# Moving the transposing DMAs of batches 2 and 3 from positions 4 and 5 to positions 8 and 9 of a step, in six steps of eight

## The chip, the cores and the metric

The kernel runs on one core of one Trainium2 chip. The metric is the device time of one execution in microseconds (us), from the inputs in device memory to the output written there. The core has a matrix engine (PE, with a separate path for its weights, PEld), a vector engine (DVE), a scalar engine (ACT), a general engine (POOL), an engine that only issues DMAs (SP), and 16 DMA engines that all queues share. Each engine works through its own instructions in the order of the program; semaphores tie the engines together. SP, POOL and ACT each issue DMAs. In this program all DMAs that transpose are issued by SP.

## The reference, cut to what matters

Two layers follow one another. The first is block-sparse attention on q, k and v of shape (4 batches, 8 heads, 768 rows, 64 columns), float32. Rows form 24 blocks of 32. A block of queries sees its own block and the two beside it, the first and the last block, and three blocks drawn for it; the first and the last block see everything.

```python
scores = scale * q @ k.T                      # scale = 1/sqrt(64)
scores = where(mask, scores, -1e9)            # mask: window, first/last block, 3 sampled blocks
attn = softmax(scores)
x = (attn @ v)                                # -> (4 * 768 tokens, 8 * 64 = 512)
```

The second is a gated feed-forward layer on the 3072 tokens, with 512 columns in and out and 1536 in the middle:

```python
xn = x / sqrt(mean(x * x) + 1e-6) * rms_g
out = (silu(xn @ w_gate) * (xn @ w_val)) @ w_out    # float32
```

## The kernel before, in words

**Batch 0** is computed densely, in three groups of 256 tokens, at the start. It plays no part in the change, except that its feed-forward work of the third group still runs when the next phase begins.

**Batches 1 to 3** are cut into 18 chunks of 128 query rows, six to a batch: chunks 0 to 5 are batch 1, 6 to 11 batch 2, 12 to 17 batch 3. The last chunk of batches 1 and 2 holds the edge blocks. The main loop has 19 steps. Step i has ten positions, 0 to 9. At a position the loop first issues the jobs listed for it (`do(n, f)` puts job f at position n) and then calls `position()`, which issues a share of the feed-forward pieces that wait in a list. So the order of all instructions is written out by hand, and an engine that waits holds up everything that stands behind it in its own order.

In step i stand, among others:

- positions 0 to 2: the product with V and the normalisation of chunk i-1 (`values`, `normalise`, L660 and L690);
- positions 1 onwards: the scores of chunk i (`scores`, L625);
- position 4: `squares` (ACT), 5: `rms_power` (POOL), 7: `x_scaled` (L714) of chunk i-1. `x_scaled` scales the chunk's rows on DVE and then lets SP issue a transposing DMA that puts them into `xg`, the moving operand of the feed-forward products (L726). Four chunks (4, 8, 16 and 17) are transposed by PE instead;
- positions 0 to 9: the gathers for chunk i+1. POOL copies sampled keys at position 0, ACT at positions 1 to 9, both on L497; DVE gathers queries and keys from position 3 on (L512 to L515 and L483 to L488); POOL issues the gathers of V by indirect DMA at position 2 (L524). All of these but the gathers of V read `KT` and `QN`, the transposed keys and queries of a batch.

**The transposed keys and queries.** `KT` and `QN` exist twice, for even and for odd batches. Those of batches 2 and 3 are made by `turn_by_dma` (L466): for a pair of heads, SP issues one transposing DMA that reads a tile of 128 partitions by 768 bf16 (192 KB) and writes a tile of the same size.

```python
def turn_by_dma(b, pr, which):
    src = (qbf if which else kbf).pop((b, pr))
    to = (QN if which else KT)[b % 2][:, 2 * pr:2 * pr + 2, :]
    nc.sync.dma_start_transpose(...)
```

There are four pairs of heads, so 8 such DMAs to a batch and 16 in all. Batch 2's stand in steps 0 to 3, batch 3's in steps 6 to 9, keys at position 4 and queries at position 5. In the profile they are `wide_k<-kbf` and `wide_k<-qbf` for batch 2, `KT<-kbf` and `QN<-qbf` for batch 3. Batch 2's are first read by the gathers for chunk 6, in step 5; batch 3's by those for chunk 12, in step 11.

**The feed-forward groups.** The 18 chunks form groups of 2, 3, 4, 4, 3 and 2, so the first chunks of groups are 0, 2, 5, 9, 13 and 16. A group's feed-forward pieces are entered at position 4 of the step two after its last chunk: group 0 (chunks 0 and 1) in step 3, group 1 (2 to 4) in step 6, group 2 (5 to 8) in step 10. The first piece is a product with `xg` (L763), so it needs the transposed rows of all the group's chunks.

**SP's queue.** SP issues, in program order: loads of V (L144), the transposes of keys and queries (L469), those of scaled rows (L726), and the stores of the output (L743, L752). A store waits for ACT's copy of the result (L797); L726 waits for DVE. The loads of keys and queries (L129 to L135), the table of V in device memory (L452) and the gathers from it (L524) are issued by POOL.

Of the kernel before, what the change touches and what calls it, by code (L numbers as in the profile page):

```python
# [18 lines left out]
def kernel(  # L19
# [64 lines left out]
    group_of = {i: g for g, m in enumerate(sgroups) for i in m}  # L84
# [51 lines left out]
    def load_kq(b, pr):  # L136
        load_one(b, pr, kbf)
        load_one(b, pr, qbf)
# [327 lines left out]
# [3 lines that stand above are left out]
        nc.sync.dma_start_transpose(out=to.rearrange("p e (c s) -> p (e c) s", s=P),  # L469
                                    in_=src.rearrange("p e x -> p (e x)"))  # L470
# [49 lines left out]
    def gather_v(i, js=range(QB)):  # L520
        b, qbs = chunks[i]
        for j in js:
            if qbs[j] not in (0, NB - 1):
                nc.gpsimd.indirect_dma_start(  # L524
                    vgs[i % 2][:, j, :], None, vtab[b][:],
                    bass.IndirectOffsetOnAxis(ap=vidx[:, qbs[j]:qbs[j] + 1], axis=0))
# [66 lines left out]
    def dense_scale(e, it):  # L593
        if it > 1:
            return
        e["xs"][it] = work.tile([P, DM], BF16, name="xs", tag="xs", bufs=3)
        nc.vector.tensor_scalar(
            out=e["xs"][it], in0=e["stage"][:, it, :], scalar1=e["rstd"][:, it:it + 1],
            scalar2=None, op0=ALU.mult)

    def dense_turn(e, part):
        shape = [P, 2, 2, P]
        t = (ps_o.tile(shape, BF16, name="tx", tag="ot") if e["grp"] == groups[1] else
             bank(shape, BF16, "tx"))
        for w in range(2):
            c = 2 * part + w
            for it in range(2):
                nc.tensor.transpose(
                    out=t[:, w, it, :], in_=e["xs"][it][:, c * P:(c + 1) * P], identity=ident)
        for w in range(2):  # L610
            c = 2 * part + w
            nc.vector.tensor_scalar(
                out=e["xg"][:, c, 0:2 * P], in0=t[:, w].rearrange("p c s -> p (c s)"),
                scalar1=rmsg[:, c:c + 1], scalar2=None, op0=ALU.mult)
# [7 lines left out]
    def bursts(i):  # L622
        return 8 if wide(i) else 4
# [36 lines left out]
    def values(i, g):  # L660
        b, qbs = chunks[i]
        op = bank([P, 512], FP32, "op")
        ops.setdefault(i, []).append(op)
        vg = vgs[i % 2].rearrange("p j (w h x) -> p j w h x", w=2, h=H)
        per = H // bursts(i)

        def mm(h, j, lhsT, rhs, n, of):
            at = (h % 4) * VW
            nc.tensor.matmul(out=op[j * BLK:(j + 1) * BLK, at:at + VW], lhsT=lhsT, rhs=rhs,  # L669
                             start=(n == 0), stop=(n == of - 1))  # L670

        for h in range(4 * g, 4 * g + 4):
            part = h // per
            ex = exs[(i, part // 4)][:, part % 4 * 512:(part % 4 + 1) * 512]
            if not wide(i):
                ex = ex.rearrange("p (h j w s) -> p h j w s", h=per, j=QB, w=2)[:, h % per]
                for w in range(2):
                    for j in range(QB):
                        mm(h, j, ex[:, j, w, :], vg[:, j, w, h, :], w, 2)
                continue  # L680
            ex = ex.rearrange("p (u w j s) -> p u w j s", w=2, j=2, s=BLK)
            for n in range(NC):
                cc, w = divmod(n, 2)
                for j in range(2):
                    mm(h, j, ex[:, cc, w, j, :], Vs[b % 2][:, 2 * cc + w, h, :], n, NC)
                if n < 2:
                    for j in range(2, QB):
                        mm(h, j, ex[:, HC, n, j - 2, :], vg[:, j, n, h, :], n, 2)
# [11 lines left out]
    def squares(i):  # L700
        ssqs[i] = work.tile([P, 1], FP32, name="ssq", tag="ssq", bufs=3)
        junk = work.tile([P, DM], BF16, name="junk", tag="junk", bufs=1)
        nc.scalar.activation(out=junk, in_=stages[i], func=AF.Square, accum_out=ssqs[i])  # L703
# [113 lines left out]
    def enter(pieces, positions):  # L817
        fill.extend(pieces)
        rate[0] = len(fill) / positions

    def enter_dense(e, positions):
        enter(ffn_pieces(e["xg"], 2, dense_store(e["grp"][1])), positions)
# [270 lines left out]
    def distance(i, n):  # L1093

        d = 0
        while True:
            n += 1
            d += 1
            if n == NPOS:
                i, n = i + 1, 0  # L1100
            if i > NCH or (i, n) in entry:
                return d

    for i in range(NCH + 1):
        jobs = {}

        def do(n, f):
            jobs.setdefault(n, []).append(f)

        b, s = divmod(i, PB)  # L1110
        b += 1
        nx = i + 1 if i + 1 < NCH else None
        if i == 0:
            do(0, late_pv)
            do(3, lambda: dense_scale(cur, 0))
            do(3, lambda: dense_scale(cur, 1))
            do(5, lambda: dense_turn(cur, 0))
            do(6, lambda: dense_turn(cur, 1))
            do(6, lambda: enter_dense(cur, distance(0, 6)))
            do(4, lambda: nc.vector.memset(Qd[1], 0.0))  # L1120
            do(3, lambda: load_kq(2, 3))
            do(7, lambda: gather_v(1, (2, 3)))
        else:
            do(0, lambda: values(i - 1, 0))
            do(0, lambda: values(i - 1, 1))
            do(1, lambda: normalise(i - 1, 0))
            do(2, lambda: normalise(i - 1, 1))
            do(4, lambda: squares(i - 1))
            do(5, lambda: rms_power(i - 1))
            do(7, lambda: x_scaled(i - 1))  # L1130
            if i == NCH:
                do(9, lambda: x_turned(i - 1))
            if i - 2 in by_pe:
                do(0, lambda: x_turned(i - 2))
        if i < NCH:
            n = bursts(i)
            for part in range(n):
                do(1 + part, lambda part=part: scores(i, part))
        if b + 1 < B and s <= NP:
            if s < NP:  # L1140
                do(9 if s == 0 else 0, lambda: cast_v(b + 1, s, act))
            if s < NP:
                do(4, lambda: turn_by_dma(b + 1, s, 0))
                do(5, lambda: turn_by_dma(b + 1, s, 1))
            if s == 0 and b == 1:
                do(8, lambda: nc.vector.memset(Vs[0][:, :, :, D:VW], 1.0))
            if s == NP:
                do(0, lambda: table(b + 1))
        if nx is not None:
            at = 6 if nx == 1 else 0  # L1150
            gk, gq = list(gather_k(nx, dve)), list(gather_q(nx, dve))
            if at == 0:
                for m, x in enumerate(gq):
                    do(3 + m * 2 // len(gq) * 2, x)
                do(4, gk[0])
                for x in gk[1:]:
                    do(6, x)
            else:
                do(at, gk[0])
                for m, x in enumerate(gk[1:]):  # L1160
                    do(at + 1 + m, x)
                for m, x in enumerate(gq):
                    do(at + 1 + m // 2, x)
            kact, kpool = sampled_k(nx, "act"), sampled_k(nx, "pool")
            for x in kpool:
                do(at, x)
            for m, x in enumerate(kact):
                do(at + (m + 1) * (NPOS - 1 - at) // len(kact), x)

            if nx > 1:  # L1170
                do(2, lambda: gather_v(nx))
        for m in range(min(6, len(by_need)) if i < 2 else 0):
            do(m, next_address)

        bl, sl = divmod(i + 2, PB)
        if 0 < bl and bl + 2 < B and sl < NP:
            do(9, lambda: load_kq(bl + 2, sl))
        bv, sv = divmod(i + 3, PB)
        if 0 < bv and bv + 2 < B and sv < NP:
            do(7, lambda: load_v(bv + 2, sv))  # L1180
        for n in range(NPOS):
            if (i, n) in entry:
                g = entry[(i, n)]
                enter(ffn_pieces(xgs[g], sizes[g], chunk_store(sgroups[g])), distance(i, n))
            for x in jobs.get(n, ()):
                x()
            position()
# [35 lines left out]
```

## Time and profile before

| | |
|---|---|
| three runs | 288.3, 306.11 and 308.67 us (median 306.11) |
| profiled execution | 288.4 us, of which the span of its instructions is 286.6 us |
| PE busy | 269.9 us, 94% of the span |
| PEld / DVE / ACT / POOL busy | 180.6 / 216.3 / 188.2 / 148.2 us |
| queue q0 (POOL's DMAs) | 32.60 MB |
| queue q1 (SP's DMAs) | 17.33 MB |

The profiled execution agrees with the lowest of the three runs, and the two others are about 18 and 20 us longer. The profile describes the first kind.

The page has six parts. Part 1 gives each engine's busy time, part 2 forty slices of the span with a digit for each engine (9 is 90% or more), part 3 the DMA queues with packets, megabytes and the time of their packets as a share of 16 engines over the span, part 4 the chain of work that ended last, part 5 the costliest groups of instructions, part 6 the DMA issues. A share of DMA engines can exceed 100%, since several packets can be in flight on one engine. Beside the page, the trace answers questions on a stretch of the span: what an engine did in order of time, what each wait ended on, how busy the engines and the DMA queues were.

### The profile page before, as it was taken

The numbers are of one execution on the slowest core, as the hardware profiler recorded it, in microseconds if no ns is written. First come the engines' busy times: TensorE is split into PE (matmuls) and PEld (weight loads), VectorE is DVE, ScalarE is ACT, GpSimd is POOL, SyncE is SP. The second block draws the span as 40 slices with busy tenths as digits, with TensorE's granted clock in tenths as the row PEclk, the third lists the DMA queues.
The fourth block names the chain that finished last, engine by engine and source line by source line (L and its number), as shares of the span: only waits on it lengthen the run. The fifth ranks groups of instructions, "written<-read, shape, count | busy, mean of one in ns | idle before, by whom it ended". The sixth has DMA issues, their size and how long they took to land.

```text
span 286.6 us, 9580 instructions
## 1 busy us (share of the span) xinstructions
PE 269.9 (94%) x3675; PEld 180.6 (63%) x3703; DVE 216.3 (75%) x596; ACT 188.2 (66%) x451; POOL 148.2 (52%) x244
## 2 busy tenths in 40 slices
PE   7898999898999989799999999999999999999995
PEld 6586896587667658566655555554545556664783
DVE  7788889678989959966999679795599941784580
ACT  4896786588488777568968759567747484533331
POOL 8857244568487575886888736628722320101000
PEclk9999999999999999999999999999999999999999
DMA  7999999999999999999999997417832252100102
GB/s 129 279 226 202 205 208 269 271 223 345 194 239 197 146 244 268 235 236 292 222 202 209 204 315 204 115 60 212 205 98 71 65 163 75 39 2 37 74 2 73
DMA packets 58417, 50.57 MB, mean 176 GB/s; under 512 B 36272, under 2 KB 50372, under 8 KB 58372
## 3 DMA queue, kind: packets, MB, share of 16 engines
q0 software_dynamic: 29376, 32.60, 56.2%
q1 hardware_dynamic: 28932, 17.33, 27.5%
q8 instruction: 29, 0.48, 0.7%
q14 instruction: 16, 0.13, 0.1%
q10 hardware_dynamic: 64, 0.03, 0.0%
HBM read 46.45 MB, written 8.83 MB: 193 GB/s over the span
## 4 chain that ended last, share of the span: by engine, by line
PE 58%; DVE 21%; DMA 10%; issue 4%; ACT 3%; POOL 2%; DVEq 0%; ACTq 0%; POOLq 0%
PE gp L763 16%; PE yp L792 15%; PE vp L774 15%; DVE hps L782 5%; DVE u L778 5%; DMA gain<-in_moe_rms_g_dram 5%; PE op L669 3%; PE st L539 3%; PE st L646 2%; DMA kbf<-in_k_dram 2%; DMA xg<-xs 2%; PE op L548 2%; DMA vraw<-in_v_dram 2%; DVE xs L724 2%; DVE stage L696 1%
## 5 line engine op out<-in xcount | busy, mean ns | idle before, releaser
L524 POOL DMA_INDIRECT vg<-vtab,vidx x66 | 66.2, 1002 | 41.0 <-PE op L669 23.8
L763 PE MATMUL gp<-xg,wg 128*128 128x256 bf16 (+2 forms) x426 | 80.5, 307 | 3.0 <-DVE stage L696 1.3
L774 PE MATMUL vp<-xg,wv 128*128 128x256 bf16 (+2 forms) x429 | 80.1, 308 | 2.3 <-DVE u L778 0.9
L767 ACT ACTIVATE th<-gp 128x256 bf16<-128x256 f32 (+2 forms) x108 | 49.8, 461 | 41.6 <-PE gp L763 37.3
L778 DVE SCALAR_TENSOR_TENSOR u<-th,gp 128x256 bf16<-128x256 bf16 (+2 forms) x108 | 54.6, 505 | 21.6 <-ACT th L767 21.1
L792 PE MATMUL yp<-wo,hps 128*128 128x512 bf16 (+1 forms) x284 | 69.0, 370 | 1.7 <-DVE hps L782 0.5
L782 DVE TENSOR_TENSOR hps<-u,vp 128x256 bf16<-128x256 bf16 (+2 forms) x108 | 55.1, 510 | 11.2
L654 ACT ACTIVATE ex<-st 128x512 bf16<-128x512 f32 x84 | 50.4, 600 | 16.0 <-PE st L646 10.8
L763 PEld LDWEIGHTS <-wg 128*128 128x128 bf16 x432 | 40.0, 98 | 21.6 <-issue 1.7
L774 PEld LDWEIGHTS <-wv 128*128 128x128 bf16 x432 | 40.0, 98 | 20.8 <-issue 2.9
L792 PEld LDWEIGHTS <-hps 128*128 128x128 bf16 x300 | 26.2, 98 | 22.0 <-DVE hps L782 1.4
L542 ACT ACTIVATE ex<-st 128x768 bf16<-128x768 f32 x42 | 33.3, 815 | 5.4 <-PE st L539 5.1
L797 ACT ACTIVATE yo<-yp 128x512 f32<-128x512 f32 (+1 forms) x25 | 14.6, 583 | 21.9 <-PE yp L792 21.8
L707 POOL TENSOR_TENSOR ssq<-ssq,eps 128x1 f32<-128x1 f32 x18 | 4.1, 226 | 40.6 <-ACT junk L703 40.4
L539 PE MATMUL st<-wide_q,wide_k 88*128 88x256 bf16 x144 | 23.2, 272 | 1.3 <-DVE wide_q L351 1.1
L669 PEld LDWEIGHTS <-ex 128*32 128x32 bf16 x1344 | 13.5, 95 | 6.4 <-issue 6.3
L696 DVE TENSOR_TENSOR stage<-op,rz 128x256 bf16<-128x256 f32 x36 | 15.3, 425 | 1.2
L539 PEld LDWEIGHTS <-wide_k 88*128 88x128 bf16 x144 | 13.0, 98 | 5.1 <-DVE wide_q L351 1.8
L669 PE MATMUL op<-vg,ex 128*32 128x66 bf16 x1056 | 15.3, 195 | 0.0
L646 PEld LDWEIGHTS <-kg 128*128 128x128 bf16 x256 | 11.8, 98 | 5.2 <-issue 0.3
L646 PEld LDWEIGHTS <-wide_q 128*128 128x128 bf16 x224 | 10.5, 98 | 5.6 <-issue 0.5
L646 PE MATMUL st<-Qd,kg 128*128 128x64 bf16 x256 | 13.0, 193 | 0.1
(152 smaller groups left out, 357.3 us busy)
## 6 DMA issues: line engine op xcount, KB each, us to landing
out_dram<-yo SPq DMA_DIRECT2D x20, 256.0 KB
vraw<-in_v_dram SPq DMA_DIRECT2D x12, 384.0 KB
kbf<-in_k_dram POOLq DMA_DIRECT2D x15, 192.0 KB, 6.2
vtab<-Vs POOLq DMA_DIRECT2D x3, 792.0 KB
qbf<-in_q_dram POOLq DMA_DIRECT2D x12, 192.0 KB, 12.3
vraw<-in_v_dram POOLq DMA_DIRECT2D x4, 384.0 KB, 6.8
wg<-in_moe_w_gate_dram POOLq DMA_DIRECT2D x4, 384.0 KB
wv<-in_moe_w_val_dram POOLq DMA_DIRECT2D x4, 384.0 KB
```

Source lines behind the costliest of these rows:

```text
L524: nc.gpsimd.indirect_dma_start(vgs[i % 2][:, j, :], None, vtab[b][:], bass.IndirectOffsetOnAxis(ap=vidx[:, qbs[j]:qbs[j] + 1], axis=0))
L539: nc.tensor.matmul(out=at[:, e], lhsT=KT0[0:KR, h, jt * P:(jt + 1) * P], rhs=QT0[0:KR, h, c0 * P:(c0 + 2) * P], start=True, stop=True)
L542: nc.scalar.activation(out=ex[:, 3 * part:3 * (part + 1), :], in_=at[:, 0:3], func=AF.Exp, scale=SCALE)
L646: nc.tensor.matmul(out=st[:, at:at + UN], lhsT=kgs[i % 2][:, h, j, :], rhs=q[:, :, j * HB:(j + 1) * HB], start=True, stop=True)
L654: nc.scalar.activation(out=ex.rearrange("p (u s w) -> p u s w", s=n, w=2), in_=st.rearrange("p (u w s) -> p u s w", s=n, w=2), func=AF.Exp ...
L669: nc.tensor.matmul(out=op[j * BLK:(j + 1) * BLK, at:at + VW], lhsT=lhsT, rhs=rhs, start=(n == 0), stop=(n == of - 1))
L763: nc.tensor.matmul(out=gp[:, 0:tg], lhsT=wg[:, c, f * P:(f + 1) * P], rhs=xg[:, c, 0:tg], start=(c == 0), stop=(c == KD - 1))
L767: nc.scalar.activation(out=th[:, 0:tg], in_=gp[:, 0:tg], func=AF.Tanh, scale=0.5)
L774: nc.tensor.matmul(out=vp[:, 0:tg], lhsT=wv[:, c, f * P:(f + 1) * P], rhs=xg[:, c, 0:tg], start=(c == 0), stop=(c == KD - 1))
L778: nc.vector.scalar_tensor_tensor(out=u[:, 0:tg], in0=th[:, 0:tg], scalar=1.0, in1=gp[:, 0:tg], op0=ALU.add, op1=ALU.mult)
L782: nc.vector.tensor_tensor(out=hps[f][:, 0:tg], in0=u[:, 0:tg], in1=vp[:, 0:tg], op=ALU.mult)
L792: nc.tensor.matmul(out=yp, lhsT=hps[f][:, tt * P:(tt + 1) * P], rhs=wo[:, f, lo:hi], start=(f == 0), stop=(f == NF - 1))
```

## The change

The position n of a step's two transposing DMAs was 4 (keys) and 5 (queries). It becomes 8 and 9, except in steps whose chunk i is the first of a feed-forward group other than group 0 (the comparison takes chunk 0 as not the first, since it compares it with itself). Of the eight steps that hold such DMAs, steps 2 and 9 keep 4 and 5; steps 0, 1, 3, 6, 7 and 8 change.

```diff
             if s < NP:
-                do(4, lambda: turn_by_dma(b + 1, s, 0))
-                do(5, lambda: turn_by_dma(b + 1, s, 1))
+
+                n = 4 if group_of[i] != group_of[i - 1 if i else 0] else 8
+                do(n, lambda: turn_by_dma(b + 1, s, 0))
+                do(n + 1, lambda: turn_by_dma(b + 1, s, 1))
```

Nothing is added or removed: the same instructions run on every engine. On PE, DVE, ACT and POOL their order is the same, too. On SP the order becomes, with K and Q for the transposes of a step, xs for L726 and V for a load of V:

| step | before | after |
|---|---|---|
| 0 | K, Q, store, store | store, K, store, Q |
| 1 | K, Q, xs(0) | xs(0), K, Q |
| 2 | K, Q, xs(1) | the same |
| 3 | store, store, K, Q, xs(2), V | store, store, xs(2), V, K, Q |
| 6 | K, Q, xs(5), V | xs(5), V, K, Q |
| 7 | K, Q, xs(6) | xs(6), K, Q |
| 8 | K, Q, xs(7) | xs(7), K, Q |
| 9 | K, store, Q, store, store | the same |

Read downwards, the order between xs(0) and xs(1) becomes K, Q of step 1 and K, Q of step 2, where it was K, Q of step 2 alone; and K, Q of step 8 come directly ahead of K of step 9.

## The prediction

> **What bounds the kernel now.** I began with the page's span, engine lines and DMA queues.
>
> ```profile
> span 286.6 us, 9580 instructions
> PE 269.9 (94%) x3675; PEld 180.6 (63%) x3703; DVE 216.3 (75%) x596; ACT 188.2 (66%) x451; POOL 148.2 (52%) x244
> DMA  7999999999999999999999997417832252100102
> ```
>
> PE is busy for 269.9 of 286.6 us, so nothing can win more than 16.7 us. The DMA digits stand at 9 from the second slice to the 24th (slices of 7.2 us, so to about 172 us). That is the stretch in which all the moved DMAs lie. So I asked for the engines' busy time from the start of step 0 of the main loop (about 66 us) to there:
>
> ```profile
> 66.00:172.00 106.00, 99.39 (x1661) 68.10 (x1667) 87.56 (x242) 79.04 (x220) 75.62 (x125) 1.00 1.19 236
> ```
>
> The columns are the stretch, its length, busy us of PE, PEld, DVE, ACT and POOL, the granted clock, the DMA share and GB/s. PE idles 106.0 - 99.4 = 6.6 us here, and a DMA share of 1.19 leaves the DMA engines no room. PE sets the end, with a full DMA system beside it: a moved transfer does not cost PE anything by itself, but it changes which transfer lands first. So the next question is which landings anybody waits for. The view of line L469 (keys and queries) and of L726 (scaled rows) lists who waited:
>
> ```profile
> L469 SPq DMA_TRANSPOSE wide_k<-kbf x4: 1245/1350/1787, 72.3 to 105.9; - x4
> L469 SPq DMA_TRANSPOSE KT<-kbf x4: 1227/1264/1878, 133.0 to 155.9; - x4
> who waited for it (us, times):
> ```
>
> ```profile
> L726 SPq DMA_TRANSPOSE xg<-xs x14: 1188/1194/1722, 91.4 to 232.9; - x14
> who waited for it (us, times):
>   PEld L763: 0.8, 1
>   PE gp L763: 0.7, 1
> ```
>
> The first list is empty under its heading: nobody is seen to wait for the transposes that move. Of the fourteen transposes of scaled rows, one is waited for, once, by 0.7 us of PE. It is that of chunk 1, the last of group 0, as the chain of waits and PE in order of time show:
>
> ```profile
> 99.50 0.66 DVE xs L724
> ...
> 100.19 5.48 DMA xg<-xs
> ```
>
> ```profile
> 105.72 0.61 PE L763 MATMUL gp<-xg,wg 128*128 128x256 bf16 x4 [0.69 <-DMA xg<-xs]
> ```
>
> DVE scales the rows, SP issues at 100.19, the transfer lands 5.48 us later, and the first product of group 0 starts at 105.72 after 0.69 us of idle PE. This transfer has no slack left. Whatever delays it delays PE one for one, and behind that product stand, in PE's order, the rest of step 3 and, through L767 and L778, ACT's and DVE's work on it.
>
> **The change, part by part.** It removes and adds no instruction; only SP's order differs. SP around the critical transfer, before:
>
> ```profile
> 82.44 1.37 SPq L469 DMA_TRANSPOSE wide_k<-kbf  x1
> 83.92 1.31 SPq L469 DMA_TRANSPOSE wide_k<-qbf  x1
> 91.45 1.19 SPq L726 DMA_TRANSPOSE xg<-xs  x1
> 92.73 1.25 SPq L469 DMA_TRANSPOSE wide_k<-kbf  x1
> 94.07 1.33 SPq L469 DMA_TRANSPOSE wide_k<-qbf  x1
> 100.19 1.19 SPq L726 DMA_TRANSPOSE xg<-xs  x1
> ```
>
> The pair at 82.44 and 83.92 is step 1's, that at 92.73 and 94.07 step 2's. Step 2's is not held by its position: SP takes it as soon as the scaled rows of chunk 0 (91.45) are issued. After the change step 1's pair stands behind 91.45 too. So SP issues four in a row, from 92.73 at about 1.35 us each: 92.73 + 4 x 1.35 = 98.1. That is before 100.19, so the issue of chunk 1's rows is not late. SP's issue time costs nothing, covered by the 4.8 us (95.40 to 100.19) in which SP had only waited for DVE. With an issue of over 1.86 us each ((100.19 - 92.73) / 4) that cover would be gone.
>
> *Step 1, the pair that is now ahead of chunk 1's rows.* Two transfers of 192 KB that used to run from 82 us on now run between 93 and 105 us. Had the DMA engines idle time there, this would cost nothing:
>
> ```profile
> 91.00:92.00 1.00, 0.66 (x12) 0.51 (x10) 0.90 (x3) 0.92 (x3) 1.00 (x1) 1.00 0.55 199
> 92.00:93.00 1.00, 1.00 (x16) 0.83 (x14) 0.90 (x3) 0.33 (x3) 0.69 (x2) 1.00 0.34 76
> 93.00:105.70 12.70, 10.98 (x167) 7.05 (x165) 10.09 (x30) 8.97 (x26) 8.34 (x13) 1.00 1.09 165
> ```
>
> They are only slack from 91 to 93 us (shares of 0.55 and 0.34), before the pair can be issued; from 93 to the landing the share is 1.09. So I count the pair's whole transfer time. Its price, from the queues in two stretches and over the span (packets, MB, share of 16 engines), the first from 75.9 to 79.1 us, where q1 runs almost alone, the second from 95 to 105 us, where POOL's gathers of V run beside it, the last from the page:
>
> ```profile
> q1 hardware_dynamic: 1670, 0.52, 121.6%
> ```
>
> ```profile
> q0 software_dynamic: 265, 0.92, 70.7%
> q1 hardware_dynamic: 1663, 0.40, 35.5%
> ```
>
> ```profile
> q1 hardware_dynamic: 28932, 17.33, 27.5%
> ```
>
> A pair is 2 x 192 KB = 0.39 MB. By the queue's mean it takes 0.275 x 286.6 = 78.8 us for 17.33 MB, so 1.8 us. In the first stretch it is 1.216 x 3.2 = 3.9 us for 0.52 MB, so 2.9 us. In the second, 10 us passed while 0.40 MB went through, so up to 9.8 us if gathers share all of it. I take 2.9 us: the first stretch holds such a pair, and the gathers that share the second are the same in number after the change, so they are already in the 5.48 us. Chunk 1's rows would land at 105.67 + 2.9 = 108.6 us: **+2.9 us**, with ends of 0 and 9.8.
>
> [...]
>
> *Step 0.* Its pair went out at 72.3 us (the first start in L469's row), ahead of two stores; it now stands between and behind them.
>
> ```profile
> 79.19 3.17 SPq L743 DMA_DIRECT2D out_dram<-yo  x2
> ...
> 111.68 0.53 SPq L144 DMA_DIRECT2D vraw<-in_v_dram  x1
> ```
>
> That is 7 to 10 us later. It takes the place that step 1's had in the DMA queues, is read only in step 5, and nothing behind it is urgent before 91.45: 0 us.
>
> *Step 3.* Its pair was issued from 105.9 on (the last start in L469's row) and now follows chunk 2's rows and a load of V (111.68 above), which come some 2 us earlier; nobody waits for them. The pair goes out some 5 to 6 us later, near 112, and later still by step 1's 2.9, as everything else. Who needs it first are POOL's and ACT's copies of sampled keys for chunk 6, then DVE's copies:
>
> ```profile
> 116.25 1.04 POOL L497 COPY kg<-wide_k 128x128 bf16 x4
> 118.12 0.29 ACT L497 COPY kg<-wide_k 128x128 bf16 x1
> 121.90 0.83 DVE L512 COPY Qd<-wide_k 64x512 bf16<-64x512 bf16 x2
> ```
>
> With the 5.48 us of the nearest transpose it lands near 117.5 to 119: after POOL's start, about at ACT's, before DVE's. POOL would wait 1 to 3 us. POOL works at 75.6 of 106 us in this phase and can take that; queued behind are its gathers of V, needed two steps on. If ACT waited, its exponentials (L654) and with them PE would. Bounds 0 and 3 us; I take 0, as ACT's time is met.
>
> *Steps 6 and 7* move behind rows of chunks 5 and 6, whose group enters only in step 10. No consumer is nearer than step 11: 0 us.
>
> *Step 8.* Its pair now goes out directly ahead of step 9's keys. The queue and its first users before:
>
> ```profile
> 154.65 1.19 SPq L726 DMA_TRANSPOSE xg<-xs  x1
> 155.94 1.23 SPq L469 DMA_TRANSPOSE KT<-kbf  x1
> 160.43 1.26 SPq L469 DMA_TRANSPOSE QN<-qbf  x1
> ```
>
> ```profile
> 166.90 1.00 POOL L497 COPY kg<-KT 128x128 bf16 x4
> 172.80 0.30 ACT L497 COPY kg<-KT 128x128 bf16 x1
> 174.55 0.58 DVE L512 COPY Qd<-QN 64x512 bf16<-64x512 bf16 x2
> ```
>
> Step 9's keys have about 11 us from issue to POOL's use, its queries 14 to DVE's; the pair in front takes 2.9 of that, or more, since the table of V for batch 3 passes on q0 in the same microseconds. A late landing holds POOL first (it idles before its next gathers anyway), then ACT and DVE, and DVE's copies stand in front of its work on PE's products. Bounds 0 and 2.9 us (the whole pair); I take **+1 us**.
>
> Sum: 2.9 + 1 = 3.9 us. The profiled execution took 288.4 us, so 292.3 us. That execution agrees with the lowest of the three runs (288.3), not with their median of 306.11; an execution like the upper two would carry the same 3.9 us, 310 to 312.6 us.
>
> **The rivals.** *A: the pair is hidden, not slower.* Taken out of the stretch from 84 us on, step 1's pair lets POOL's gathers land sooner, and these then leave the field to the transposes after 93 us. For it speaks that total transfer work is the same; against it, that the gathers beside the critical transfer are issued after 92 us, whatever came before. It decides if chunk 1's rows still land by about 106 us. Time: at best the 0.7 us wait goes, at worst 1.5 us come: 287.7 to 289.9.
>
> *B: the pair takes its turns with the gathers.* If q0's large packets and q1's small ones alternate, each transpose takes far longer than alone, as between 95 and 105 us, where q0 has twice q1's share. Then the pair costs about the middle of 2.9 and 9.8, some 6 us, at step 2, and 3 us at step 9: 288.4 + 9 = 297.4. It decides once chunk 1's rows land after 110 us. [...]
>
> *C: faster.* The delayed start of group 0 drains the DMA queues, and later waits on DVE and ACT shrink by more than it cost. PE's idle of 6.6 us in the phase is the ceiling: 282 to 288. No row speaks for it.
>
> *D: the move does nothing.* SP's order does change in six steps, so only A's outcome could look so.
>
> **How the numbers follow.** My forecast (291 to 294.5) gets 0.46, A 0.20, B 0.29, C 0.05. Two per cent, about what a measurement of this kernel can tell from no change, is 5.8 us, so the border is 294.2. Slower by more: B's 0.29 and 0.06 of the forecast's upper end, 0.35. Faster by more: 0.04. The rest, 0.61, is within 2%. The likeliest case alone gives 291 to 294.5. The range must also take in A and most of B, and an execution like the upper two runs: 287.5 to 313.
>
> **What would show it.** In the changed profile, four transposes of L469 should stand between those of L726 for chunks 0 and 1. The product behind chunk 1's rows (L763) should show an idle PE of 3 to 4 us before it, released by `xg<-xs`, where it was 0.69, and that transfer's latency 8 to 9 us. L497 on POOL should wait for a DMA near 119 and 168 us. I am wrong if that latency stays under 6 us (A), exceeds 10 (B), or if PE's idle time in the phase does not grow although the landing is late.

## The result, and the profile after

The changed kernel takes 306.56 us (median of 6, from 303.85 to 310.29). The kernel before, timed beside it, gave 288.3, 288.92, 290.61, 301.45, 306.11 and 308.67 us. The ratio is 1.0575 with a 95% interval of 1.0492 to 1.0659, so the change makes the kernel **slower**. Each ratio here compares only executions within 1.5% of the fastest of their kernel and so leaves the long ones out, while medians and spreads count them all: over all six, the median of before is 296.03 us.

The profiled execution took 305.27 us. Its page:

```profile
span 303.5 us, 9581 instructions
PE 276.7 (91%) x3675; PEld 183.9 (61%) x3703; DVE 217.2 (72%) x596; ACT 188.5 (62%) x451; POOL 147.6 (49%) x244
...
PE   8899999999999878999996659999999999999995
...
PEclk9999999999999999999999578999999999999999
...
L763 PE MATMUL gp<-xg,wg 128*128 128x256 bf16 (+2 forms) x426 | 82.2, 312 | 6.4 <-DMA xg<-xs 2.3
...
L669 PE MATMUL op<-vg,ex 128*32 128x66 bf16 x1056 | 16.2, 198 | 4.0 <-DMA vg<-vtab,vidx 4.0
```

The span grew by 16.9 us. PE's idle time grew from 286.6 - 269.9 = 16.7 to 303.5 - 276.7 = 26.8 us, and PE's busy time by 6.8 us for the same instructions. Most of both has one place: the digits of PE fall to 6, 6, 5 around 160 to 180 us, and the granted clock falls to 5 and 7 just behind. PE now waits there for the gathers of V (4.0 us), and at 107 us for the scaled rows (2.3 us).

The windows on both sides of that place (the stretch, its length, busy us of PE, PEld, DVE, ACT and POOL, granted clock, DMA share, GB/s), before:

```profile
145.00:165.00 20.00, 19.04 (x300) 11.43 (x302) 16.85 (x44) 15.07 (x41) 15.88 (x26) 1.00 1.21 210
165.00:185.00 20.00, 19.73 (x308) 11.01 (x310) 16.50 (x37) 13.52 (x35) 11.33 (x20) 1.00 0.76 212
```

and after:

```profile
145.00:165.00 20.00, 17.97 (x266) 10.34 (x266) 16.12 (x39) 14.26 (x39) 15.98 (x26) 1.00 1.12 146
165.00:185.00 20.00, 12.43 (x122) 6.29 (x123) 5.91 (x18) 5.23 (x12) 2.73 (x4) 0.66 1.23 190
```

From 145 to 165 us the DMA share is about the same (1.12 for 1.21), yet the DMA engines move 146 GB/s instead of 210. From 165 to 185 us every engine starves, and PE runs at a clock of 0.66.

Since PE's order is the same in both kernels, the loss can be dated by setting the same instructions side by side. PE in order of time (start, us, instruction; in brackets idle time before it and what ended it), before:

```profile
153.03 0.70 PE L669 MATMUL op<-vg,ex 128*32 128x66 bf16 x64
161.11 0.69 PE L669 MATMUL op<-vg,ex 128*32 128x66 bf16 x64
164.84 1.03 PE L763 MATMUL gp<-xg,wg 128*128 128x512 bf16 x4
...
170.12 0.70 PE L669 MATMUL op<-vg,ex 128*32 128x66 bf16 x64
```

and after:

```profile
107.76 0.61 PE L763 MATMUL gp<-xg,wg 128*128 128x256 bf16 x4 [2.27 <-DMA xg<-xs]
...
155.24 0.70 PE L669 MATMUL op<-vg,ex 128*32 128x66 bf16 x64
...
165.27 0.19 PE L669 MATMUL op<-vg,ex 128*32 128x66 bf16 x1 [0.94 <-DMA vg<-vtab,vidx]
168.48 1.04 PE L669 MATMUL op<-vg,ex 128*32 128x66 bf16 x61 [3.02 <-DMA vg<-vtab,vidx]
...
178.97 1.86 PE L763 MATMUL gp<-xg,wg 128*128 128x512 bf16 x4 [1.92 <-issue]
...
187.02 0.71 PE L669 MATMUL op<-vg,ex 128*32 128x66 bf16 x64
```

| the same instruction | before, us | after, us | late by | added |
|---|---|---|---|---|
| first product behind chunk 1's rows (L763) | 105.72 | 107.76 | 2.0 | 2.0 |
| chunk 8's product with V (L669) | 153.03 | 155.24 | 2.2 | 0.2 |
| end of chunk 9's product with V | 161.80 | 169.52 | 7.7 | 5.5 |
| first product of group 2 (L763) | 164.84 | 178.97 | 14.1 | 6.4 |
| chunk 10's product with V | 170.12 | 187.02 | 16.9 | 2.8 |

So the loss comes in three places: 2.0 us up to chunk 1's rows, 1.6 of them in the wait that was forecast; 5.5 us because the gathers of V for chunk 9, issued in step 8, land late; and 9.2 us around the start of group 2, partly waiting and partly at the low clock (four products take 1.86 us instead of 1.03). In the trace's semaphore events, chunk 7's rows, which group 2 needs, land at 178.88 us, 0.1 us before its first product; the idle 1.92 us that the row puts down to "issue" end there.

What SP did in these two places, after:

```profile
91.97 1.19 SPq L726 DMA_TRANSPOSE xg<-xs  x1
93.25 1.24 SPq L469 DMA_TRANSPOSE wide_k<-kbf  x1
94.58 1.39 SPq L469 DMA_TRANSPOSE wide_k<-qbf  x1
96.06 1.42 SPq L469 DMA_TRANSPOSE wide_k<-kbf  x1
97.57 3.28 SPq L469 DMA_TRANSPOSE wide_k<-qbf  x1
100.95 1.63 SPq L726 DMA_TRANSPOSE xg<-xs  x1
...
141.11 1.22 SPq L469 DMA_TRANSPOSE KT<-kbf  x1
142.42 1.31 SPq L469 DMA_TRANSPOSE QN<-qbf  x1
148.52 1.19 SPq L726 DMA_TRANSPOSE xg<-xs  x1
149.81 2.37 SPq L469 DMA_TRANSPOSE KT<-kbf  x1
152.27 5.30 SPq L469 DMA_TRANSPOSE QN<-qbf  x1
157.66 2.33 SPq L726 DMA_TRANSPOSE xg<-xs  x1
160.09 5.55 SPq L469 DMA_TRANSPOSE KT<-kbf  x1
165.73 11.42 SPq L469 DMA_TRANSPOSE QN<-qbf  x1
```

The five transposes issued from 149.81 to 165.73 us take 2.3 to 11.4 us each to issue, where the three ahead of them took 1.2 to 1.3 us. In before the longest issue of batch 3's eight transposes took 2.17 us. By the semaphore events, the pairs of steps 6 to 8 land 8 to 21 us after their issue (4.5 to 9.5 before), chunk 7's rows 21.2 us after it (8.25 before).

The DMA queues from 158 to 166 us (packets, MB, share of 16 engines), before:

```profile
q0 software_dynamic: 365, 1.23, 64.0%
q1 hardware_dynamic: 1483, 0.59, 45.3%
```

and after:

```profile
q0 software_dynamic: 178, 0.60, 63.7%
q1 hardware_dynamic: 1229, 0.31, 37.9%
```

At the same share of DMA time q0, which carries gathers here, moves half the megabytes. The two rows of q1 are not alike: 0.26 of the 0.59 MB in before are a store, in packets of 2048 bytes. The transposes' packets, of 256 bytes, come to 0.33 MB before and 0.31 MB after.

The traces record each packet, which shows where the time goes. Take the 23 us that follow the first gather for chunk 9, from 147 to 170 us before and from 149 to 172 us after. A gather's packet of 4224 bytes takes 464 ns in the mean where it took 268. The median is the same (173 and 174 ns): 17% of the packets, instead of 4%, take over 1 us. A transpose's packet takes 33 ns, and 37 before, so it is no slower by itself; but only 0.65 MB of such packets go out, instead of 0.91 MB. Some gather packets last far longer, then, and fewer of the transposes' get through beside them. I call this the *slow manner* below.

### The profile page after: what moved, and what is told of

Read it like the earlier page. It is cut to its first block, busy times and chain, and to the rows that moved or that the text cites. A ratio compares the mean times of both kernels' runs of the same rounds, so it can differ in the third digit from the quotient of the medians.

```text
span 303.5 us, 9581 instructions
## 1 busy us (share of the span) xinstructions
PE 276.7 (91%) x3675; PEld 183.9 (61%) x3703; DVE 217.2 (72%) x596; ACT 188.5 (62%) x451; POOL 147.6 (49%) x244
## 4 chain that ended last, share of the span: by engine, by line
PE 55%; DVE 21%; DMA 13%; issue 5%; ACT 3%; ACTq 0%; POOL 0%; DVEq 0%
PE gp L763 15%; PE vp L774 14%; PE yp L792 13%; DVE u L778 5%; DMA vg<-vtab,vidx 5%; DVE hps L782 5%; DMA gain<-in_moe_rms_g_dram 4%; PE op L669 3%; PE st L539 3%; PE st L646 2%; DMA xg<-xs 2%; PE op L548 2%; DMA vraw<-in_v_dram 2%; DVE xs L724 1%; PE unread L234 1%
## 5 line engine op out<-in xcount | busy, mean ns | idle before, releaser
L524 POOL DMA_INDIRECT vg<-vtab,vidx x66 | 65.5, 992 | 47.2 <-PE op L669 30.1
L763 PE MATMUL gp<-xg,wg 128*128 128x256 bf16 (+2 forms) x426 | 82.2, 312 | 6.4 <-DMA xg<-xs 2.3
L774 PE MATMUL vp<-xg,wv 128*128 128x256 bf16 (+2 forms) x429 | 81.2, 311 | 2.3 <-DVE u L778 0.8
L792 PE MATMUL yp<-wo,hps 128*128 128x512 bf16 (+1 forms) x284 | 70.1, 375 | 1.8 <-DVE hps L782 0.4
L654 ACT ACTIVATE ex<-st 128x512 bf16<-128x512 f32 x84 | 50.3, 599 | 26.8 <-PE st L646 22.5
L763 PEld LDWEIGHTS <-wg 128*128 128x128 bf16 x432 | 40.3, 98 | 25.9 <-issue 5.4
L669 PEld LDWEIGHTS <-ex 128*32 128x32 bf16 x1344 | 14.2, 96 | 10.8 <-issue 10.6
L669 PE MATMUL op<-vg,ex 128*32 128x66 bf16 x1056 | 16.2, 198 | 4.0 <-DMA vg<-vtab,vidx 4.0
L646 PEld LDWEIGHTS <-kg 128*128 128x128 bf16 x256 | 12.6, 101 | 8.4 <-issue 3.7
L646 PE MATMUL st<-Qd,kg 128*128 128x64 bf16 x256 | 14.0, 197 | 2.2 <-issue 2.1
```

Of the source, the lines that this page charges most:

```text
L524: nc.gpsimd.indirect_dma_start(vgs[i % 2][:, j, :], None, vtab[b][:], bass.IndirectOffsetOnAxis(ap=vidx[:, qbs[j]:qbs[j] + 1], axis=0))
L646: nc.tensor.matmul(out=st[:, at:at + UN], lhsT=kgs[i % 2][:, h, j, :], rhs=q[:, :, j * HB:(j + 1) * HB], start=True, stop=True)
L654: nc.scalar.activation(out=ex.rearrange("p (u s w) -> p u s w", s=n, w=2), in_=st.rearrange("p (u w s) -> p u s w", s=n, w=2), func=AF.Exp ...
L763: nc.tensor.matmul(out=gp[:, 0:tg], lhsT=wg[:, c, f * P:(f + 1) * P], rhs=xg[:, c, 0:tg], start=(c == 0), stop=(c == KD - 1))
L774: nc.tensor.matmul(out=vp[:, 0:tg], lhsT=wv[:, c, f * P:(f + 1) * P], rhs=xg[:, c, 0:tg], start=(c == 0), stop=(c == KD - 1))
L792: nc.tensor.matmul(out=yp, lhsT=hps[f][:, tt * P:(tt + 1) * P], rhs=wo[:, f, lo:hi], start=(f == 0), stop=(f == NF - 1))
```

## The experiments

Each group of runs had a chip of its own, with executions of the kernel before beside it:

| chip | kernel before: executions, lowest to highest, median |
|---|---|
| A | 11: 288.3 to 306.46, 297.88 |
| B | 7: 306.92 to 313.56, 311.48 |
| C | 13: 304.76 to 311.27, 307.91 |
| D | 7: 288.5 to 313.21, 301.77 |
| E | 11: 288.9 to 306.4, 301.71 |

On chips B and C the kernel before never comes under 304 us; what is lost there is told in the last section. Kernels are compared on the same chip only.

### Chip A: which half, and is it the transposing?

**Batch 2's pairs alone** are moved.

```diff
-                n = 4 if group_of[i] != group_of[i - 1 if i else 0] else 8
+                n = 8 if i in (0, 1, 3) else 4
```

> Only batch 2's pairs move (steps 0, 1 and 3); batch 3's stay at 4 and 5. Theory Q (each moved pair delays what stands behind it, and the loss of some 17 us comes from the pairs of steps 6 to 8): only the landing of chunk 1's rows is later, PE idles some 2 us more before group 0, ratio 1.005 to 1.015. Theory P (any small delay tips the transfers of steps 7 to 9 into the slow manner of the changed kernel, whichever pair causes it): most executions at 300 us or more, ratio 1.04 to 1.06, and gathers of V around step 8 that take 13 us or more to land.

302.56 us (293.2 to 308.64), ratio 1.0188, 1.008 to 1.0295. The profiled execution was a long one, 306.12 us, and it loses time from 150 us on as the changed kernel does, although batch 3's pairs stand where they stood. So this run separates little: a longer wait at chunk 1's rows (4.23 us here) costs its own price, and an execution can still fall into the slow manner later.

**Batch 3's pairs alone** are moved.

```diff
+                n = 8 if i in (6, 7, 8) else 4
```

> Only batch 3's pairs move (steps 6, 7 and 8); batch 2's stay at 4 and 5. Theory Q: steps 0 to 3 as in the kernel before (0.7 us of idle PE before group 0), and 14 to 16 us lost between 148 and 185 us: ratio 1.04 to 1.06. Theory P: about the same as with batch 2 alone, so both the same.

304.21 us (299.29 to 308.23), 1.0395, 1.0291 to 1.0499. None of the six executions comes under 299 us, while before falls to 288.3 on the same chip. Most of the loss comes from batch 3's moves.

**Step 8's pair alone** is moved.

```diff
+                n = 8 if i == 8 else 4
```

> Only step 8's pair moves, behind the rows of chunk 7 and directly ahead of step 9's keys. Theory Q: the loss comes from four transposes in a row at steps 8 and 9, so most of it stays: ratio 1.03 to 1.05, the keys of step 9 landing 15 us or more after their issue. Theory M (the loss comes from transposes of steps 6 and 7 running into gathers of V, which slows both): steps 6 and 7 are as before, so at most 2 us are lost, ratio 1.00 to 1.01.

291.21 us (288.92 to 296.44), 1.0048, 0.9987 to 1.0108. The pair directly ahead of step 9's keys costs nothing that can be measured, although these keys land late (16.2 us after their issue). The theory that this pair is the cause falls.

**The changed order with plain copies** for all 16 transposes of keys and queries; the copies have the same bytes, tiles and places in SP's order.

```diff
-        nc.sync.dma_start_transpose(out=to.rearrange("p e (c s) -> p (e c) s", s=P),
-                                    in_=src.rearrange("p e x -> p (e x)"))
+        nc.sync.dma_start(out=to, in_=src)
```

> The changed kernel with plain copies of the same tiles in place of the 16 transposes of keys and queries, so the keys and queries of batches 2 and 3 are not transposed and their scores are not those of the reference; bytes, queue and order stay. If the queued bytes matter alone: as the changed kernel, ratio 1.04 to 1.06, with gathers of V that take 13 us or more around step 8. If transposing itself matters (a transpose beside gathers slows both): the long landings go, latencies at 5 to 9 us, ratio 0.98 to 1.01.

288.31 us, and the six executions lie between 287.87 and 288.87, beside 288.3 to 306.46 for the kernel before. Both the loss and the spread are gone. The queues of this kernel from 158 to 166 us:

```profile
q0 software_dynamic: 380, 1.57, 63.9%
q1 hardware_dynamic: 702, 1.02, 33.9%
```

For about the same DMA share q0 moves 2.6 times and q1 3.3 times the megabytes of the changed kernel. Part of that is other traffic (0.72 MB of the table of V on q0, 0.30 MB of a store on q1); the gathers' own packets take 268 ns in the mean in this stretch, and 572 in the changed kernel. So neither the moved bytes nor the place in SP's queue cause the loss: that these DMAs transpose does, or that they do so in small packets, since the copies go in packets of 1536 bytes and the transposes in packets of 256. No run tells these two apart. The spread of before probably has the same cause, since it goes too; no long execution of before itself was profiled, so this is inferred.

### Chip B: is it the gathers beside them?

**Steps 6 and 7 moved** is the control of this chip.

```diff
+                n = 8 if i in (6, 7) else 4
```

> Only the pairs of steps 6 and 7 move; step 8's and batch 2's stay. If the pairs of steps 6 and 7 make the loss by meeting the gathers of V one step later than before: as with all of batch 3 moved, 299 to 308 us, ratio 1.03 to 1.06. If it takes step 8's pair ahead of step 9's keys as well: 288 to 293 us, as with step 8 alone.

330.69 us (327.21 to 335.82), 1.0572, 1.0431 to 1.0714, so the loss is there on this chip too, about 19 us. In PE's order of time it shows at group 2's start:

```profile
204.02 1.86 PE L763 MATMUL gp<-xg,wg 128*128 128x512 bf16 x4 [13.38 <-DMA xg<-xs]
```

**The changed order with plain loads in place of the gathers** of V for chunks 6 to 11: the same bytes from the first 128 rows of the table, issued by the same instruction stream.

```diff
             if qbs[j] not in (0, NB - 1):
+                if 6 <= i < 12:
+                    nc.gpsimd.dma_start(out=vgs[i % 2][:, j, :], in_=vtab[b][0:P, :])
+                    continue
```

> The changed kernel with each gather of V of batch 2 (chunks 6 to 11) replaced by a plain load of the same size from the table's first 128 rows, same queue, same place; the output of batch 2 is then not the reference's. If transposes are slow beside any traffic of POOL's queue: as the changed kernel, all executions at 300 us or more. If it takes indirect gathers: executions near 290 to 293 us, and landings around step 8 of 5 to 9 us.

303.52 us (302.15 to 306.43), 0.9811, 0.9706 to 0.9916: no loss, and even less than before on that chip.

**The changed order without the gathers** of V for chunks 8 to 11.

```diff
-            if nx > 1:
+            if nx > 1 and not 7 < nx < 12:
                 do(2, lambda: gather_v(nx))
```

> The changed kernel without the gathers of V of chunks 8 to 11 (their rows are those of chunks 6 and 7, so the output of these chunks is not the reference's). If gathers of V beside transposes are the cause: the 10 us of idle PE between 148 and 185 us go, executions at 288 to 293 us, transposes of step 8 landing after 5 to 8 us. If the partner is another (loads of keys and queries, the table of V): still 300 us or more.

307.72 us (306.29 to 309.82), 0.9939, 0.9842 to 1.0036: no loss either. So, as far as these runs show, the loss needs both: transposes on q1 and *indirect* gathers on q0. Plain loads of the same size, in the same number of packets, beside the transposes don't cause it; the mean packet of 4224 bytes takes 231 ns from 149 to 180 us there. Two limits remain. The changed kernel itself was not run on this chip, where steps 6 and 7 stand for it. And the plain loads read the same 128 rows each time, so scattered rows and the indirect issue are not told apart.

**The order of before, with the last two pairs of batch 3 transposed by PE** and copied by ACT.

```diff
+        if b == 3 and pr > 1:
+            t = bank([P, 2, HC, P], BF16, "tqk")
+            for e in range(2):
+                for cc in range(HC):
+                    nc.tensor.transpose(out=t[:, e, cc, :], in_=src[:, e, cc * P:(cc + 1) * P],
+                                        identity=ident)
+            act(out=to.rearrange("p e (c s) -> p e c s", s=P), in_=t)
+            return
```

> The kernel before, with batch 3's last two pairs (steps 8 and 9) transposed by PE and copied out by ACT in place of four transposing DMAs. PE gets 24 transposes of 128x128, at 0.083 us each 2 us. If transposing DMAs that meet gathers of V are what makes some executions long: all executions at 289 to 293 us. If not: as many executions at 300 us or more as the kernel before has.

313.24 us (310.96 to 313.71), 1.0097, 1.0004 to 1.0191. The hoped-for 289 to 293 us did not come. The four transposes taken away here are not what keeps the kernel before above 300 us in every execution on this chip, and PE's added work cost 1%.

### Chip C: which step?

**Step 6's pair alone.**

```diff
+                n = 8 if i == 6 else 4
```

> Only step 6's pair moves, behind chunk 5's rows; four transposes in a row follow then at steps 6 and 7, and steps 8 and 9 are as before. Theory S (the slow manner needs several steps in which a pair goes out together with a burst of four gathers of V): one more such step than before, so within 1% of the kernel before, long executions about as often. Theory F (four transposes in a row, ahead of scaled rows that are needed, are the loss): chunk 6's rows are late, but nobody waits for them before step 10: also within 1%.

320.31 us (307.04, 319.48, 321.15, 323.02). Both theories expected no loss; it is 12 us in the median, though one of the four executions shows none. In the profiled execution PE waits 5.6 us for scaled rows at group 2's start.

**Step 7's pair alone.**

```diff
+                n = 8 if i == 7 else 4
```

> Only step 7's pair moves, behind chunk 6's rows, so that four transposes in a row stand directly ahead of chunk 7's rows, which are the last transposed rows of group 2. Theory F: these rows land after 13 us or more and PE waits for them, 3 to 10 us over the kernel before. Theory S: as with step 6 alone, within 1%.

308.49 us, 1.0024, 0.9969 to 1.0079: no loss (nine executions from 304.96 to 309.33, one at 325.23). To issue a transpose of queries in steps 6 to 9, SP needed up to 8.80 us (median 3.22) with step 6 moved, and up to 2.03 us (median 1.57) with step 7 moved.

**The changed kernel again**, unaltered, on this chip.

> The changed kernel once more, as the reference of this call. Every theory: 5 to 6% over the fast executions of the kernel before, if that has fast ones on this chip; chunk 7's rows land 15 to 21 us after their issue, transposes of steps 7 and 8 after 13 us or more.

308.5, 313.49, 318.32 and 324.53 us, median 315.9 beside 307.91 for before. The lowest of the four lies within before's spread.

**The changed kernel with chunk 7's rows transposed by PE**, which takes away the transfer that group 2 waits for.

```diff
-    by_pe = [*sgroups[-1], sgroups[1][-1], sgroups[2][-1]]
+    by_pe = [*sgroups[-1], sgroups[1][-1], *sgroups[2][-2:]]
```

> The changed kernel with chunk 7's rows transposed by PE (four transposes, 0.33 us), so that group 2 waits for no DMA later than chunk 6's rows. If the wait for chunk 7's rows is most of the loss: 8 us or more under the changed kernel of this call. If the late gathers of V and late keys hold PE anyway: at most 4 us under it.

312.67 to 323.9 us, median 321.11: no help. PE's waits from 150 to 205 us are now for the gathers:

```profile
PE op L669 <- DMA vg<-vtab,vidx: 9.0, 3, 6.8
```

The late rows are therefore one victim of the slow manner, not its cause; when they no longer hold PE, the gathers do.

### Chip D: is step 6 needed, and how does it act?

Step 6's pair used to go out between two bursts of gathers. POOL's gathers for chunks 8 and 9 (first and last of four each) and SP's transposes of the keys of steps 6, 7 and 8, put together in order of time, before:

```profile
133.04 1.88 SPq L469 DMA_TRANSPOSE KT<-kbf  x1
137.44 1.07 POOL L524 DMA_INDIRECT vg<-vtab,vidx  x1 [0.17 <-PE st L646]
138.86 1.23 SPq L469 DMA_TRANSPOSE KT<-kbf  x1
141.37 1.18 POOL L524 DMA_INDIRECT vg<-vtab,vidx  x1 [0.30 <-DVE hps L782]
...
146.85 1.06 POOL L524 DMA_INDIRECT vg<-vtab,vidx  x1 [0.17 <-issue]
147.62 1.30 SPq L469 DMA_TRANSPOSE KT<-kbf  x1
150.76 0.95 POOL L524 DMA_INDIRECT vg<-vtab,vidx  x1 [0.30 <-PE vp L774]
```

and the gathers after, with the keys of steps 6 and 7 at 141.11 and 149.81 us (shown above):

```profile
139.65 1.07 POOL L524 DMA_INDIRECT vg<-vtab,vidx  x1 [0.17 <-PE st L646]
143.58 1.18 POOL L524 DMA_INDIRECT vg<-vtab,vidx  x1 [0.30 <-DVE hps L782]
...
149.05 1.06 POOL L524 DMA_INDIRECT vg<-vtab,vidx  x1 [0.17 <-issue]
152.95 0.95 POOL L524 DMA_INDIRECT vg<-vtab,vidx  x1 [0.30 <-DVE u L778]
```

Before, step 6's pair is issued at 133.0 and 135.0 us, ahead of chunk 8's burst; after, it stands in the middle of that burst. But before, step 7's pair stood there, at the same distance: keys 1.4 us behind the burst's first gather in before, 1.5 us after. The same holds for chunk 9's burst, with step 8's pair before and step 7's after (0.8 us in both). So meeting these bursts is not new. New is that step 6's pair is not done by then, and that one pair more is still to be sent beside gathers: four from chunk 8's burst on, where there were three.

The late landings begin in the second of these bursts. Chunk 8's gathers land within 9.8 us of their issue (8.5 before), chunk 9's after 11.2 to 15.5 us (7.2 to 8.7 before).

**All moves but step 6's.**

```diff
+                n = 8 if i in (0, 1, 3, 7, 8) else 4
```

> All moves of the change but that of step 6. Theory N (the loss needs step 6's pair to go out into the burst of gathers of step 7, one pair more that meets a burst): only the 2 us before group 0 are left, ratio 1.00 to 1.015, transposes of steps 7 to 9 landing in 4 to 10 us. If the number of moved pairs decides: 1.03 to 1.06.

294.34 us (293.25 to 295.2), 1.02, 1.0124 to 1.0276. The wait at chunk 1's rows is 3.79 us in the profiled execution, against 0.69 in before's:

```profile
109.40 1.04 PE L763 MATMUL gp<-xg,wg 128*128 128x256 bf16 x4 [3.79 <-DMA xg<-xs]
```

and nothing from 150 us on waits for a DMA. So without step 6's move some 6 of 17 us remain, 3.1 us of them at the place of the prediction.

**Steps 7 and 8 alone.**

```diff
+                n = 8 if i in (7, 8) else 4
```

> Only the pairs of steps 7 and 8 move. Theory N: three pairs meet bursts, as before, but in two bursts in place of three: ratio 0.98 to 1.005, executions no more spread than before's. If any two moved pairs of batch 3 do it: 1.03 to 1.06.

287.86, 288.49, 290.18 and, the profiled one, 306.19 us; 1.0012, 0.9913 to 1.011. The three agree with the lowest of before. The long one shows the slow manner without step 6's move: from 150 to 205 us PE waits 10.7 us in all for the gathers of V, 5.2 us at the longest.

**The changed kernel without one burst**, the gathers of V for chunk 8, which meet step 6's pair.

```diff
-            if nx > 1:
+            if nx > 1 and nx != 8:
```

> The changed kernel without the one burst of gathers for chunk 8, issued in step 7 (chunk 8 then takes chunk 6's rows, so its output is not the reference's). Theory N: step 6's pair meets no burst, the loss goes but for the 2 us before group 0: ratio 1.00 to 1.015, transposes of steps 7 to 9 landing in 4 to 10 us. Theory V (the load of V ahead of step 6's pair decides): the loss stays, 1.03 to 1.06.

294.03 us (290.54 to 295.14), 1.0151, 0.9979 to 1.0323. One burst of four gathers less takes away most of the loss, about what leaving step 6's pair in its place does. As before has a pair in this burst too, this shows that less traffic helps, not that this meeting is the cause. The unaltered changed kernel was not run on this chip; the loss is that of its other runs.

**Step 6's pair at position 7**, still behind chunk 5's rows but ahead of the load of V that stands between them in the changed kernel.

```diff
-                do(n, lambda: turn_by_dma(b + 1, s, 0))
-                do(n + 1, lambda: turn_by_dma(b + 1, s, 1))
+                do(7 if i == 6 else n, lambda: turn_by_dma(b + 1, s, 0))
+                do(7 if i == 6 else n + 1, lambda: turn_by_dma(b + 1, s, 1))
```

> The changed kernel with step 6's pair directly behind chunk 5's rows and ahead of step 6's load of V. Theory V: the loss goes, ratio 1.00 to 1.015. Theory N: the pair still meets the burst of step 7, so 1.03 to 1.06, with landings of 13 us or more in steps 7 and 8.

291.27, 296.38, 300.25 and 301.94 us, median 298.31: between the two theories. In this kernel's profiled execution (291.27 us) the pair meets the same burst without a collapse. Whether the load of 384 KB ahead of the pair does part of the harm is not shown by four executions that spread over 11 us; what tips an execution stays open.

### Chip E: a version that keeps the good part

**Steps 3, 7 and 8 moved.** This leaves out step 1 (the wait at chunk 1) and step 6.

```diff
+                n = 8 if i in (3, 7, 8) else 4
```

> Only the pairs of steps 3, 7 and 8 move. If step 1's pair is what held PE before group 0: that wait is 1 to 2 us at most, as in the kernel before. If the moves of steps 3, 7 and 8 are what empties the queues: every execution at 287 to 291 us, median under that of the kernel before. If the queues were emptied by PE's wait in step 3: long executions of 300 us or more stay, as with steps 7 and 8 alone.

288.31, 288.44, 289.66, 292.95, 295.75 and 301.79 us, median 291.3 beside 301.71 for before's eleven (288.9 to 306.4). No wait at chunk 1.

**The same with step 0.**

```diff
+                n = 8 if i in (0, 3, 7, 8) else 4
```

> As the one above, with step 0's pair moved too. Step 0's pair then goes out directly ahead of step 1's, behind the stores: 0 to 1 us more than without it; whether long executions stay comes out as above.

Median 292.35 us, seven of eight from 288.43 to 296.06, one at 303.95, which was the profiled one. It has the slow manner at another place, and chunk 1's rows were the victim (17.6 us from issue to landing):

```profile
118.58 1.04 PE L763 MATMUL gp<-xg,wg 128*128 128x256 bf16 x4 [10.97 <-DMA xg<-xs]
```

In the median of all executions both are below the kernel before on this chip, where the changed kernel was not run; their best executions are no faster than before's. With six and eight executions that spread over 13 and 15 us, the gain is that long executions look rarer, and it is not shown more firmly than that.

## Why the prediction was wrong

The forecast was 292.3 us and no more than a small loss; measured were 306.56. The range held this only through its upper end, which stood for another reason, the long executions of before; that is luck.

**Step 1, +2.9 us: right in its place and kind.** The four L469 stand between the two L726; the wait before the first product of group 0 is 2.27 us (0.69 before), released by `xg<-xs`. That is +1.6 us, about half of the forecast; on chips A and D, in the profiled executions of the four kernels that move step 1's pair as transposes, it is +2.3 to +3.5 (and +1.2 in a long execution without that move). The landing took 6.8 us from issue, not 8 to 9. The assumption that SP's issue is covered nearly failed: the fourth transpose took 3.28 us to issue, and chunk 1's rows were issued at 100.95, right behind it.

**Step 3, 0 us: right.** POOL's copy of sampled keys near 118 us starts without a wait:

```profile
118.31 1.04 POOL L497 COPY kg<-wide_k 128x128 bf16 x4
```

**Step 8, +1 us: right, as far as the runs can tell.** Moved alone, the pair costs 1.0048 (0.9987 to 1.0108), which is about 1.4 us and not clear of nothing. In that kernel's profiled execution step 9's keys land 16.2 us after their issue, and POOL waits for them:

```profile
177.21 1.00 POOL L497 COPY kg<-KT 128x128 bf16 x4 [8.32 <-DMA KT<-kbf]
```

ACT then waits 2.2 us and DVE 1.3 us, in the order that the prediction named, and little of it reaches PE. In the changed kernel POOL waits 6.21 us for the same keys, within the slow manner.

**Steps 6 and 7, 0 us: this is the step that failed.** "No consumer is nearer than step 11" is true of the moved transposes themselves: nobody waited for step 6's. The sentence counted a moved transfer by who reads it and not by what is in flight beside it. Step 7's move is indeed free (1.0024). Step 6's alone costs 12 us in the median, and with it left out the ratio falls from 1.0575 to 1.02. It leaves one pair more to be sent beside the bursts of gathers, and the traffic behind it, the gathers for chunk 9 and the rows of chunk 7, pays 5.5 and 9.2 us. The prediction's sentence that a moved transfer "changes which transfer lands first" was therefore too weak: the move also changed how long the others take. How it does so is open, since before sends a pair at the same place in the same two bursts and its profiled execution shows no harm.

**The price of a pair** came from a stretch in which q1 ran almost alone, with the upper end of 9.8 us from a mixed stretch. For step 1 the 2.9 us fit, at +1.6 to +3.5. In steps 6 to 8 no price of the pair itself describes the loss, which falls on the gathers and rows around it.

**Rival B** (turns between the queues) named the right partners. Its places, step 2 and step 9, and its 9 us were wrong: the large losses came in between. No run shows that the large and the small packets alternate. What the traces show is that a gather's packet grows from 268 to 464 ns in the mean, while 0.65 MB of the transposes' packets go out instead of 0.91 MB, at 33 ns each instead of 37. Something in the pairing of transposes and indirect gathers makes the gathers' packets longer; no run here shows what it is.

**Rivals A, C and D** fell: the pair was not hidden, nothing got faster, and the order of SP did change.

What stays open is the point from which the slow manner sets in. It comes per execution: the same kernel gave 287.86 and 306.19 us. Step 6's move makes it the rule. With one burst of gathers less four executions took 290.54 to 295.14 us, and plain copies took the loss away altogether in six executions. One reading is a count: from chunk 8's burst on three pairs go out beside gathers in before, and four with step 6's moved. It fits most runs, but not the kernel with the pair ahead of the load of V, and no run tests it by itself.

## What to carry to other kernels

When a transfer is moved, look at what will be in flight beside it, and not only at its consumer: of two pairs of transposing DMAs, one could be moved behind other traffic for nothing (step 7's), and the other, 8 us later than before, brought the slow manner (step 6's). A DMA share that stays while the GB/s fall, and issue times on SP that grow from 1.3 to 5 or 11 us, were the signs here. A kernel whose executions spread by 6% without a change of code may stand close to such an edge, and its fastest execution is then a poor base for a forecast.

## What the runs showed of the hardware that was not expected

- **Beside transposing DMAs an indirect gather's packets took much longer in some executions.** From 149 to 180 us the mean packet of 4224 bytes took 342 to 581 ns in the eight profiled executions with the slow manner there (429 after). In the eleven others with such packets it took 221 to 323 ns (260 before, 227 with plain copies in place of the transposes of keys and queries).
- **Around PE's waits the granted clock was low, too.** After, PE waits 3.0, 2.1 and 1.9 us up to 168.5, 175.9 and 179.0 us. The granted clock was 0.50 twice for 6.8 us, from 167.6 and from 177.8 us on, and so from within the first and the third of these waits. Behind the third the same four products took 1.86 us instead of 1.03. The two stretches, after, with the granted clock third from the end:

```profile
167.60:174.40 6.80, 5.09 (x92) 3.40 (x92) 3.79 (x14) 1.38 (x3) 1.98 (x2) 0.50 1.31 246
177.80:184.60 6.80, 5.63 (x14) 2.03 (x15) 2.04 (x3) 2.02 (x7) 0.75 (x2) 0.50 1.42 200
```

  What brings the clock down is not shown.
- **The chips differed.** On chips B and C the kernel before never came under 304 us, on A, D and E its lowest were 288.3 to 288.9 us. A profile from chip C (step 7's pair moved, 308.41 us) shows a stretch in which the granted clock is 0.79:

```profile
91.00:107.00 16.00, 11.80 (x153) 8.87 (x151) 12.09 (x32) 10.19 (x33) 7.47 (x16) 0.79 0.71 122
```

  PE waits 2.8 us for an exponential of ACT just there. This is not the slow manner (the DMA share is 0.71, and SP issues its transposes there in 1.2 to 1.4 us); its cause is open.
